# Loading four x tiles ahead of the v weights, projecting v of two of them early, and summing tile means on two engines, in the head of a one-core kernel

## The chip, the cores and the metric

One core of a Trainium2 chip runs the kernel. The metric is device time in microseconds (us). The names of the engines are: PE (TensorE, matrix products), ACT (ScalarE), DVE (VectorE), POOL (GpSimd), SP (SyncE, which here only issues transfers). Transfers are issued from two queues, SP's and ACT's.

## The reference

The input x has 2048 tokens of 512 numbers. It is normalised per token, and three things are added: x itself, a linear attention, and a bilinear gated layer.

```
xn  = (x - mean(x)) / sqrt(var(x) + 1e-5)
A   = linear_attention(xn @ wqkv, features = softmax(+-(q|k) @ w_phi), 32 heads of 16) @ wo
B   = ((xn @ w_gate) * (xn @ w_up)) @ w_down          # 512 -> 1792 -> 512
out = x + A + B
```

All inputs are bfloat16. The key and query parts of `wqkv` are folded with `w_phi` on the chip; the v part (`wv` below, 512 x 512) is used as it is.

## The kernel before: the parts that matter

x is worked on in 16 tiles of 128 tokens. A tile is centred (mean subtracted), transposed on PE, copied out of PSUM (the evacuation), and then multiplied with weights. For the first four tiles (ND = 4) the division by the standard deviation is deferred to later stages, so only the mean is on the path to the first matrix product. `sc.pin` keeps the recorded order on each engine; a small list scheduler orders everything else.

The transfers of the head:

```python
    sc.pin = True
    load_x(0, 2)                    # SP: x tiles 0 and 1
    load_v(SP, 0)                   # SP: rows 0-255 of wv ("half 0")
    load_x(2, 2)                    # SP: x tiles 2 and 3
    load_gu(SP, 0, (1,))            # SP: first slice of w_up
    act(sbf("lnv", 0, 1), eps_f, ["eps"], ["pace"])
    load_v(ACT, 1)                  # ACT: wv half 1
    load_gu(ACT, 0, (0,))           # ACT: first slice of w_gate
    load_gu(SP, 1)
    # ... w_phi, the transposed key weights, x tiles 4-7, more slices
```

The work of the head, in order (for one engine this order is kept):

```python
    warm(7)                         # matmuls on constants
    warm(2, 512, [("x", 0)])
    sc.pin = True
    ln_moments(0)                   # DVE: bn_stats + bn_aggr, gives the mean of tile 0
    ln_mean(1)                      # ACT: sum of tile 1 by accumulation
    ln_center(0, 2)                 # DVE
    ln_center(1, 2)
    x_transpose(0, 2, 0, 2)         # PE transposes, ACT or DVE copies out of PSUM
    x_transpose(0, 3, 1, 2)
    x_transpose(1, 4, 0, 2, DVE)
    x_transpose(1, 5, 1, 2, DVE)
    v_matmul(0, 0)                  # v of tile 0: half 0 of wv, then half 1
    v_matmul(1, 1)
    # ... ln_moments(2), ln_mean(3), centre tiles 2 and 3
    g0a()                           # quarter units of gate and up: 4 matmuls of 256 columns each
    x_transpose(2, 2)
    g1a()
    x_transpose(3, 3)
    u0a()
    u1a()
    sc.pin = False
    # ... the main loop follows; it computes v of tiles 2 to 15
```

The softmax here doesn't subtract the row's maximum and nothing guards it: scores larger than these inputs give would overflow.

Of the kernel before, what the change touches and what calls it, by code (L numbers as in the profile page):

```python
# [7 lines left out]
ACTF = mybir.ActivationFunctionType  # L8
# [7 lines left out]
H = 32  # L16
# [103 lines left out]
def _build(nc, es, A_x, A_wqkv, A_w_phi, A_wo, B_w_gate, B_w_up, B_w_down, out):  # L120
# [3 lines left out]
    def alloc(name, nelem, at=None):  # L124
        if at is not None:
            layout[name] = at
            return
        off = (cur[0] + 31) // 32 * 32
        layout[name] = off
        cur[0] = off + nelem  # L130
# [14 lines left out]
    alloc("ek", RK * 1024)  # L145
    alloc("vs", RK * H * HC)
    alloc("eq", RQ * 1024)
    alloc("o", 3 * 512)
    alloc("g", 4 * 512)
    alloc("ostg", 3 * 512)  # L150
# [9 lines left out]
    alloc("nbias", 2 * NT)  # L160
    alloc("lnv", 2 * NT)
    alloc("mu", 2 * ND)
    alloc("nrstd", 2 * ND)
    alloc("r2", 2 * ND)
    alloc("rpr", 2 * RK * 32)
# [20 lines left out]
    def sbf(name, lo, n):  # L186
        off = layout[name] + 2 * lo
        return arena[:, off:off + 2 * n].bitcast(F32)

    def bank(b, lo=0, n=512):  # L190
        return psum[:, b * 512 + lo:b * 512 + lo + n]
# [6 lines left out]
    def act(out_ap, in_ap, reads, writes, func=ACTF.Copy, scale=1.0, bias=None, accum=None):  # L198
        kw = {} if bias is None else {"bias": bias}
        if accum is not None:  # L200
            kw["accum_out"] = accum
        n = out_ap.free_size()
        return sc.step(ACT, lambda e: e.activation(out=out_ap, in_=in_ap, func=func, scale=scale, **kw),  # L203
                       reads, writes, 130.0 + 0.833 * n)

    def dve(fn, reads, writes, n, rate=1.04):
        return sc.step(DVE, fn, reads, writes, 140.0 + rate * n)
# [25 lines left out]
    def x_tile(t):  # L233
        return sb("x", t * 512, 512)
# [9 lines left out]
    def load_x(t0, n, eng=SP):  # L244
        o = sb("x", t0 * 512, n * 512).rearrange("p (t d) -> p t d", t=n)
        i = rows(x_flat, t0, n)
        sc.dma(eng, lambda e: e.dma_start(o, i), [], [("x", t) for t in range(t0, t0 + n)], n * 131072)
# [16 lines left out]
    def load_gu(eng, s, which=(0, 1)):  # L264
        lo, n = SLICES[s]
        sl = slice(lo, lo + n)
        for k in which:
            v, src = ((wg_v, B_w_gate), (wu_v, B_w_up))[k]
            load_w(eng, v[:, :, sl], src[:, sl].rearrange("(q p) f -> p q f", p=128), (("wg", "wu")[k], s),
                   1024 * n)  # L270

    def load_v(eng, h):
        i = A_wqkv[h * 256:(h + 1) * 256, 1024:1536].rearrange("(q p) j -> p q j", p=128)
        load_w(eng, wv_v[:, 2 * h:2 * h + 2, :], i, ("wv", h), 262144)
# [7 lines left out]
    pool(c_fn, [], ["const"], 300)  # L282

    sc.pin = True
    load_x(0, 2)
    load_v(SP, 0)
    load_x(2, 2)
    load_gu(SP, 0, (1,))
    act(sbf("lnv", 0, 1), eps_f, ["eps"], ["pace"])
    load_v(ACT, 1)  # L290
    load_gu(ACT, 0, (0,))
    load_gu(SP, 1)
    load_w(SP, wphi_v, bass.AP(tensor=A_w_phi.tensor, offset=A_w_phi.offset, ap=[[16, 128], [2048, NQ], [1, 16]]),
# [55 lines left out]
    def xn_tile(t):  # L349
        return sb("xn", (t % 4) * 512, 512)  # L350
# [8 lines left out]
    def ln_moments(t):  # L359
        dve(lambda e: e.bn_stats(stats_v[:, t, 0:6], x_tile(t)), [("x", t)], [("st", t)], 512)  # L360
        dve(lambda e: e.bn_aggr(mv_v[:, t, :], stats_v[:, t, 0:6]), [("st", t)], [("mv", t)], 1)  # L361
# [8 lines left out]
    def ln_stats(t0, n):  # L370
# [3 lines left out]
        ln_rstd(t0, n)  # L374
        sc.prio = 1

    def ln_mean(t):
        act(xn_tile(t), x_tile(t), [("x", t)], [("mu", t)], scale=1.0 / 512.0, accum=mu[:, t:t + 1])

# [53 lines left out]
    def features(name, t, w, b=None):  # L433
        s = t % (RK if w else RQ)
        e_v = sb(name, s * 1024, 1024).rearrange("p (h k f) -> p h k f", h=H, k=2)
        b = misc_bank() if b is None else b
        mm(bank(b), [(xnT(q, t * 128, 128), Wp_v[:, w, q, :]) for q in range(NQ)],
           xk(t) + [("Wp", w, q) for q in range(NQ)], b)
        src = bank(b).rearrange("p (h f) -> p h f", h=H)
        late = t < ND  # L440
        act(e_v[:, :, 0, :], src, [("ps", b)] + late * [("rstd", t)], [(name, s, 0)], func=ACTF.Exp,
            scale=rstd[:, t:t + 1] if late else 1.0)
        act(e_v[:, :, 1, :], src, [("ps", b)] + late * ["nrstd"], [(name, s, 1)], func=ACTF.Exp,
            scale=nrstd[:, t:t + 1] if late else -1.0)
        sr = t % 8 if w == 0 else 8 + t % 4
        sm = sums_v[:, sr]
        dve(lambda e: e.tensor_reduce(out=sm, in_=e_v, axis=AX.X, op=ALU.add),  # L447
            [(name, s, 0), (name, s, 1)], [("sums", sr)], 1024)
        rs = rs_v[:, s]
        if w == 1:  # L450
            dve(lambda e: e.reciprocal(out=rs, in_=sm), [("sums", sr)], [("rs", s)], 64, 6.5)  # L451
        else:
            dve(lambda e: e.reciprocal(out=rs[:, :, 1], in_=sm[:, :, 1]), [("sums", sr)], [("rs", s)], 32, 6.5)  # L453
        rat = rat_v[:, s]
        pool(lambda e: e.tensor_tensor(out=rat, in0=sm[:, :, 0], in1=rs[:, :, 1], op=ALU.mult),  # L455
             [("sums", sr), ("rs", s)], [("rat", s)], 32)
        pool(lambda e: e.tensor_tensor(out=e_v[:, :, 1, :], in0=e_v[:, :, 1, :],  # L457
                                       in1=rat[:, :, None].to_broadcast([128, H, 16]), op=ALU.mult),
             [(name, s, 1), ("rat", s)], [(name, s, 1)], 512)

    def vs_tile(t):
        return sb("vs", (t % RK) * H * HC, H * HC).rearrange("p (h c) -> p h c", h=H)

    def v_matmul(t, b, hs=(0, 1)):
        for h in hs:
            mm(bank(b), [(xnT(q, t * 128, 128), wv_v[:, q, :]) for q in (2 * h, 2 * h + 1)],
               ([("xnT", t, h)] if t < 2 else [("xnT", t)]) + [("wv", h)], b, start=h == 0, stop=h == 1)

    rpr_v = sbf("rpr", 0, RK * 32).rearrange("p (r h) -> p r h", r=RK)

    def v_scale(t, b):
        s = t % RK
        rp, key = rs_v[:, s, :, 0], ("rs", s)
        pool(lambda e, rp=rp: e.tensor_copy(out=vs_tile(t)[:, :, 16], in_=rp), [("rs", s)], [("vz", s)], 32)  # L474
        if t < ND:
            pr = rpr_v[:, s]
            pool(lambda e, rp=rp: e.tensor_scalar(out=pr, in0=rp, scalar1=rstd[:, t:t + 1], scalar2=None,
                                                  op0=ALU.mult), [("rs", s), ("rstd", t)], [("rpr", s)], 32)
            rp, key = pr, ("rpr", s)
        dve(lambda e: e.tensor_tensor(out=vs_tile(t)[:, :, 0:16], in0=bank(b).rearrange("p (h f) -> p h f", h=H),  # L480
                                      in1=rp.unsqueeze(2).to_broadcast([128, H, 16]), op=ALU.mult),
            [("ps", b), key], [("vs", s)], 512)

    def kv_acc(t):
        s = t % RK
# [150 lines left out]
    def warm(n, w=512, after=()):  # L636
        def fn(e):
            ins = None
            for _ in range(n):
                ins = e.matmul(bank(7, 0, w), lhsT=nc.const_aps.tensor(1.0, (128, 128), BF16),  # L640
                               rhs=nc.const_aps.tensor(1.0, (128, w), BF16), start=True, stop=True)
            return ins
        sc.step(PE, fn, after, [("ps", 7)], n * w * 0.8)

    warm(7)
    warm(2, 512, [("x", 0)])
    sc.pin = True
    ln_moments(0)
    ln_mean(1)
    ln_center(0, 2)  # L650
    ln_center(1, 2)
    x_transpose(0, 2, 0, 2)
    x_transpose(0, 3, 1, 2)
    x_transpose(1, 4, 0, 2, DVE)
    x_transpose(1, 5, 1, 2, DVE)
    v_matmul(0, 0)
    v_matmul(1, 1)
    ln_moments(2)
    ln_mean(3)
    ln_center(2)  # L660
    ln_center(3)
    ln_moments(1)
    ln_moments(3)
    (g0a, u0a, g0b, u0b), gate0 = up_unit(*ups.pop(0), pairs, 2)
    (g1a, u1a, g1b, u1b), gate1 = up_unit(*ups.pop(0), pairs, 2)
    g0a()
    x_transpose(2, 2)
    g1a()
    x_transpose(3, 3)
    u0a()  # L670
    u1a()
    sc.pin = False
    ln_deferred()
# [34 lines left out]
    for t in range(NT + 3):  # L708
        if t < NT:
            features("ek", t, 1)  # L710
        if t % 2 == 0 and 4 + t < NT:
            ln_stats(4 + t, 2)
        if t > 0:
            up()
        x_next(t + 4)
        late_loads(t)
        if 2 <= t - 1 < NT:
            b = misc_bank()
            v_matmul(t - 1, b)
            v_scale(t - 1, b)  # L720
        if t < 2:
            v_scale(t, t)
        else:
            up()
            if t >= 3:
                kv_acc(t - 3)
            if t < NT + 1:
                up()
        if 7 < t < 12:
            w_fold(0, t - 8)  # L730
        if t >= NT - 3:
            features("eq", t - NT + 3, 0)
            q_transpose(t - NT + 3)
# [164 lines left out]
```

## Time and profile before

221.38 us is the median of six runs (221.30 to 221.69). The traced run was taken apart from these and took 221.54 us.

| quantity | value | where it is read |
|---|---|---|
| PE busy | 98% of the span | the page |
| chain of waits on PE | 96% | the page |
| x tiles 0-1 have landed | 4.28 us | landings in the trace |
| first transpose | 5.59 us | timeline of PE |
| x tiles 2-3 have landed | 7.34 us | landings in the trace |
| PE without a gap from | 8.73 us | single matmuls in the trace |
| start of the last matmul | 217.29 us | single matmuls in the trace |

These are two lines of the page of the kernel before: the busy time of each engine, and the engines' shares of the chain that ended last.

```profile
PE 214.4 (98%) x1251; PEld 105.0 (48%) x1275; DVE 141.3 (64%) x245; ACT 86.2 (39%) x162; POOL 53.6 (24%) x119
PE 96%; DMA 2%; issue 1%; DVE 1%
```

PE is the bottleneck, nearly from end to end. (About two dozen matmul records are missing in this trace, so the sum of PE's busy time is not used for anything finer.) The question is where the last few per cent lie. The next lines are the chain of waits of the kernel before, in order of time: start, length, and what the chain ran through (pieces of under 0.1 us are left out).

```profile
0.79 3.49 DMA arena<-in_A_x_dram
4.30 0.71 DVE arena L360
5.03 0.19 DVE arena L361
5.25 0.30 DVE arena L385
5.59 0.87 PE ps L417 x8
6.46 2.22 PE ps L222 x12
8.73 0.40 PE ps L417 x4
```

Until 5.59 us the chain is a transfer (x tiles 0-1), bn_stats, its aggregation, and one half of the centring. From then on it stays on PE. The timeline of PE alone shows the gaps (start, busy time, line, shapes, number of matmuls; in brackets the idle time before them):

```profile
5.59 0.87 PE L417 MATMUL ps<-arena 128*128 128x128 bf16 x8 [0.66 <-DVE arena L385]
6.35 2.34 PE L222 MATMUL ps<-arena 128*128 128x512 bf16 x12
8.73 0.40 PE L417 MATMUL ps<-arena 128*128 128x128 bf16 x4
8.96 0.60 PE L222 MATMUL ps<-arena 128*128 128x256 bf16 x4
```

L417 is a transpose, L222 any product with a weight. The 0.2 us hole before 8.73 does not show as a wait in brackets, because the modelled ends of matmuls run on; it shows when the starts of single matmuls are compared. In a gapless stretch they follow each other by 216 ns (512 columns), 109 ns (256) or 56 ns (128).

That gives a way to count the head. Call *head cost* the time at which PE starts to run without a gap, less the real matmuls it has already done by then, at these spacings. Before: 8.73 us less 8 transposes, 8 v matmuls and 4 quarter matmuls (0.45 + 1.73 + 0.44 = 2.61 us) is 6.12 us.

### The profile page before, as it was taken

The numbers are of one execution on the slowest core, as the hardware profiler recorded it, in microseconds if no ns is written. First come the engines' busy times: TensorE is split into PE (matmuls) and PEld (weight loads), VectorE is DVE, ScalarE is ACT, GpSimd is POOL, SyncE is SP. The second block draws the span as 40 slices with busy tenths as digits, with TensorE's granted clock in tenths as the row PEclk, the third lists the DMA queues.
The fourth block names the chain that finished last, engine by engine and source line by source line (L and its number), as shares of the span: only waits on it lengthen the run. The fifth ranks groups of instructions, "written<-read, shape, count | busy, mean of one in ns | idle before, by whom it ended". The sixth has DMA issues, their size and how long they took to land.

```text
span 219.8 us, 3293 instructions
## 1 busy us (share of the span) xinstructions
PE 214.4 (98%) x1251; PEld 105.0 (48%) x1275; DVE 141.3 (64%) x245; ACT 86.2 (39%) x162; POOL 53.6 (24%) x119
## 2 busy tenths in 40 slices
PE   6999999999999999999999999999999999999995
PEld 1664444444444444544444444544454444454453
DVE  2766999876546654675486565797766777445341
ACT  4568774787343435333445525531122211000000
POOL 3030553332022202220241422224332222200000
DMA  6999715298200000000002220343764545342221
GB/s 182 295 302 297 198 43 121 59 336 185 49 0 0 0 3 0 0 0 3 0 0 48 49 47 4 71 74 76 163 144 100 118 106 115 87 102 73 61 61 49
DMA packets 47104, 19.90 MB, mean 91 GB/s; under 512 B 37488, under 2 KB 46448, under 8 KB 47088
## 3 DMA queue, kind: packets, MB, share of 16 engines
q1 hardware_dynamic: 46288, 19.16, 36.0%
q10 hardware_dynamic: 800, 0.52, 0.8%
q8 instruction: 10, 0.16, 0.3%
q14 instruction: 6, 0.05, 0.1%
HBM read 8.67 MB, written 2.10 MB: 49 GB/s over the span
## 4 chain that ended last, share of the span: by engine, by line
PE 96%; DMA 2%; issue 1%; DVE 1%
PE ps L222 91%; PE ps L539 2%; PE ps L492 2%; DMA arena<-in_A_x_dram 2%; PE ps L333 1%; PE ps L417 1%; DVE arena L360 0%; DVE arena L385 0%; DVE arena L621 0%; DVE arena L361 0%
## 5 line engine op out<-in xcount | busy, mean ns | idle before, releaser
L222 PE MATMUL ps<-arena 128*128 128x512 bf16 (+3 forms) x938 | 204.8, 371 | 1.3
L222 PEld LDWEIGHTS ps<-arena 128*128 128x128 bf16 x962 | 90.8, 98 | 98.2 <-ACT arena L203 0.2
L203 ACT ACTIVATE arena<-ps 128x512 bf16<-128x512 f32 (+2 forms) x114 | 63.0, 593 | 87.3 <-PE ps L222 74.3
L597 DVE TENSOR_TENSOR arena<-ps,arena 128x512 bf16<-128x512 f32 x56 | 38.5, 687 | 21.8 <-PE ps L222 18.0
L447 DVE TENSOR_REDUCE arena<-arena 128x64 f32<-128x1024 bf16 x32 | 38.5, 1213 | 20.9 <-ACT arena L203 20.9
L457 POOL TENSOR_TENSOR arena<-arena 128x512 bf16<-128x512 bf16 x32 | 33.9, 1060 | 1.3
L455 POOL TENSOR_TENSOR arena<-arena 128x32 f32<-128x32 f32 x32 | 8.6, 268 | 91.2 <-DVE arena L451 50.8
L621 DVE TENSOR_TENSOR arena<-ps,arena 128x512 bf16<-128x512 f32 (+2 forms) x13 | 8.5, 650 | 21.5 <-PE ps L222 21.5
L203 ACT ACTIVATE arena<-arena 128x512 bf16<-128x512 bf16 (+3 forms) x29 | 14.4, 508 | 5.8 <-DMA arena<-in_A_x_dram 2.8
L360 DVE BATCH_NORM_STATS2 arena<-arena 128x6 f32<-128x512 bf16 x16 | 10.4, 674 | 5.0 <-DMA arena<-in_A_x_dram 4.9
L203 ACT ACTIVATE arena<-ps,arena 128x512 bf16<-128x512 f32 x16 | 10.1, 685 | 5.7 <-PE ps L222 5.7
L560 DVE TENSOR_TENSOR arena<-ps,arena 128x512 bf16<-128x512 f32 x16 | 11.1, 691 | 0.6
L480 DVE TENSOR_TENSOR arena<-ps,arena 128x512 bf16<-128x512 f32 x16 | 10.3, 643 | 0.0
L451 DVE RECIPROCAL arena<-arena 128x64 f32<-128x64 f32 x16 | 8.4, 533 | 0.0
L492 PEld LDWEIGHTS ps<-arena 128*128 128x128 bf16 x128 | 6.2, 97 | 3.8
L539 PEld LDWEIGHTS ps<-arena 128*128 128x128 bf16 x128 | 6.2, 97 | 3.8
L397 POOL TENSOR_SCALAR arena<-arena 128x1 f32<-128x1 f32 x12 | 3.0, 269 | 17.7 <-ACT arena L203 17.7
L539 PE MATMUL ps<-arena 128*128 128x68 bf16 x128 | 6.7, 194 | 0.0
L492 PE MATMUL ps<-arena 128*128 128x68 bf16 x128 | 6.7, 194 | 0.0
L559 DVE RECIPROCAL arena<-arena 128x32 f32<-128x32 f32 x16 | 5.6, 353 | 0.5
L453 DVE RECIPROCAL arena<-arena 128x32 f32<-128x32 f32 x16 | 5.4, 344 | 0.2
L474 POOL CAST arena<-arena 128x32 bf16<-128x32 f32 x16 | 5.2, 322 | 0.0
(30 smaller groups left out, 34.0 us busy)
## 6 DMA issues: line engine op xcount, KB each, us to landing
out_dram<-arena SPq DMA_DIRECT2D x15, 128.0 KB, 1.7
arena<-in_B_w_down_dram SPq DMA_DIRECT2D x1, 1792.0 KB, 8.0
arena<-in_A_x_dram SPq DMA_DIRECT2D x3, 512.0 KB, 3.7
arena<-arena SPq DMA_TRANSPOSE x44, 2.8
arena<-in_B_w_gate_dram SPq DMA_DIRECT2D x1, 640.0 KB, 8.9
arena<-in_B_w_up_dram SPq DMA_DIRECT2D x1, 640.0 KB, 10.0
arena<-in_A_x_dram SPq DMA_DIRECT2D x2, 256.0 KB, 4.6
arena<-in_B_w_gate_dram SPq DMA_DIRECT2D x1, 512.0 KB, 5.4
```

The costliest lines, as they stand in the source:

```text
L203: return sc.step(ACT, lambda e: e.activation(out=out_ap, in_=in_ap, func=func, scale=scale, **kw), reads, writes, 130.0 + 0.833 * n)
L222: ins = e.matmul(out_ap, lhsT=l, rhs=r, start=start and i == 0, stop=stop and i == npair - 1, **kw)
L360: dve(lambda e: e.bn_stats(stats_v[:, t, 0:6], x_tile(t)), [("x", t)], [("st", t)], 512)
L447: dve(lambda e: e.tensor_reduce(out=sm, in_=e_v, axis=AX.X, op=ALU.add), [(name, s, 0), (name, s, 1)], [("sums", sr)], 1024)
L455: pool(lambda e: e.tensor_tensor(out=rat, in0=sm[:, :, 0], in1=rs[:, :, 1], op=ALU.mult), [("sums", sr), ("rs", s)], [("rat", s)], 32)
L457: pool(lambda e: e.tensor_tensor(out=e_v[:, :, 1, :], in0=e_v[:, :, 1, :], in1=rat[:, :, None].to_broadcast([128, H, 16]), op=ALU.mult), [ ...
L480: dve(lambda e: e.tensor_tensor(out=vs_tile(t)[:, :, 0:16], in0=bank(b).rearrange("p (h f) -> p h f", h=H), in1=rp.unsqueeze(2).to_broadca ...
L492: ins = e.matmul(bank(c // 4, (c % 4) * CW, CW), lhsT=ek[:, c * 128:(c + 1) * 128], rhs=vs[:, c * CW:(c + 1) * CW], start=(t == 0 and c % ...
L539: ins = e.matmul(bank(b0 + c // 4, (c % 4) * CW, CW), lhsT=ph[:, c, :], rhs=kvz_v[:, c, :], start=True, stop=True)
L560: dve(lambda e: e.tensor_tensor(out=o_tile(t).rearrange("p (b h f) -> p b h f", b=2, f=16), in0=nd[:, :, :, 0:16], in1=w_v[:, r].unsqueeze ...
L597: dve(lambda e: e.tensor_tensor(out=hT_v[:, ft, sg * 512:(sg + 1) * 512], in0=bank(bu), in1=g, op=ALU.mult), [("ps", bu), ("g", s)], [("hT ...
L621: dve(lambda e, ps=ps, stg=stg, cs=cs: e.tensor_tensor(out=stg, in0=ps, in1=x_tile(t)[:, cs], op=ALU.add), [("ps", bk), ("x", t)], [("ostg ...
```

## The change

Its intent is to start PE's real work earlier and give it more to do early. The first x transfer is cut in two, on two queues; all four first x tiles go ahead of `wv`; the mean of a tile is summed half on ACT and half on DVE; and v of tiles 2 and 3 is projected in the head, where it is copied raw in float32 into a buffer that is free until late, and scaled in the loop.

```diff
-    load_x(0, 2)
-    load_v(SP, 0)
+    load_x(0, 1)
+    load_x(1, 1, ACT)
     load_x(2, 2)
+    load_v(SP, 1)
     load_gu(SP, 0, (1,))
     act(sbf("lnv", 0, 1), eps_f, ["eps"], ["pace"])
-    load_v(ACT, 1)
+    load_v(ACT, 0)
     load_gu(ACT, 0, (0,))
@@ new helpers
+    def ln_mean_split(t):      # ACT sums columns 256-511, DVE columns 0-255
+    def ln_center_split(t):    # DVE, two halves, subtracts both part means
+    def ln_center_whole(t):
+    def v_keep(t, b):          # ACT: PSUM -> float32 in SBUF
@@ head
-    warm(2, 512, [("x", 0)])
+    warm(1, 512, [("x", 0)])
-    ln_moments(0)
-    ln_mean(1)
-    ln_center(0, 2)
-    ln_center(1, 2)
+    ln_mean_split(0)
+    ln_center_split(0)
+    ln_mean_split(1)
+    ln_center_split(1)
+    ln_mean_split(2)
     x_transpose(0, 2, 0, 2)
     x_transpose(0, 3, 1, 2)
+    warm(1, 256)
     x_transpose(1, 4, 0, 2, DVE)
     x_transpose(1, 5, 1, 2, DVE)
+    warm(1, 256)
+    ln_center_whole(2)
+    ln_mean(3)
+    ln_center(3)
     v_matmul(0, 0)
-    v_matmul(1, 1)
-    ... statistics of tiles 0 to 3
+    v_matmul(1, 1, (0,))
+    x_transpose(2, 6)
+    v_matmul(1, 1, (1,))
+    for t in range(ND):
+        ln_moments(t)
     g0a()
-    x_transpose(2, 2)
-    g1a()
-    x_transpose(3, 3)
-    u0a()
+    x_transpose(3, 7)
+    v_matmul(2, 2)
+    v_keep(2, 2)
+    u0a()
+    v_matmul(3, 3)
+    v_keep(3, 3)
+    g1a()
     u1a()
@@ loop: v of tiles 2 and 3 is scaled from the kept copy, no matmul there
```

More of the change, by code (lines that the diff above doesn't have):

```diff
@@ L147, in _build @@
     alloc("eq", RQ * 1024)
+    alloc("vraw", 2 * 1024, at=layout["eq"])
     alloc("o", 3 * 512)
@@ L162, in _build @@
     alloc("mu", 2 * ND)
+    alloc("mua", 2 * ND)
     alloc("nrstd", 2 * ND)
@@ L375, in ln_stats @@
         sc.prio = 1
+    mua = sbf("mua", 0, ND)
+    def ln_mean_split(t):
+        act(xn_tile(t)[:, 256:], x_tile(t)[:, 256:], [("x", t)], [("mu", t)], scale=1.0 / 512.0,
+            accum=mu[:, t:t + 1])
+        dve(lambda e: e.tensor_scalar(out=xn_tile(t)[:, :256], in0=x_tile(t)[:, :256], scalar1=1.0 / 512.0,
+                                      scalar2=0.0, op0=ALU.mult, op1=ALU.add, accum_out=mua[:, t:t + 1]),
+            [("x", t)], [("mua", t)], 256)
+    def ln_center_split(t):
+        for h in range(2):
+            hs = slice(h * 256, (h + 1) * 256)
+            dve(lambda e, hs=hs: e.tensor_scalar(out=xn_tile(t)[:, hs], in0=x_tile(t)[:, hs], scalar1=mua[:, t:t + 1],
+                                                 scalar2=mu[:, t:t + 1], op0=ALU.subtract, op1=ALU.subtract),
+                [("x", t), ("mua", t), ("mu", t)], [("xn", t, h)], 256, 0.27)
+    def ln_center_whole(t):
+        dve(lambda e: e.tensor_scalar(out=xn_tile(t), in0=x_tile(t), scalar1=mua[:, t:t + 1],
+                                      scalar2=mu[:, t:t + 1], op0=ALU.subtract, op1=ALU.subtract),
+            [("x", t), ("mua", t), ("mu", t)], [("xn", t, 0)], 512, 0.27)
     def ln_mean(t):
@@ L440, in features @@
         late = t < ND
-        act(e_v[:, :, 0, :], src, [("ps", b)] + late * [("rstd", t)], [(name, s, 0)], func=ACTF.Exp,
+        over = [("vraw", 2), ("vraw", 3)] if name == "eq" and t < 2 else []
+        act(e_v[:, :, 0, :], src, [("ps", b)] + late * [("rstd", t)], [(name, s, 0)] + over, func=ACTF.Exp,
             scale=rstd[:, t:t + 1] if late else 1.0)
@@ L467, in v_matmul @@
                ([("xnT", t, h)] if t < 2 else [("xnT", t)]) + [("wv", h)], b, start=h == 0, stop=h == 1)
+    def v_keep(t, b):
+        raw = sbf("vraw", (t - 2) * 512, 512)
+        act(raw, bank(b), [("ps", b)], [("vraw", t)])
     rpr_v = sbf("rpr", 0, RK * 32).rearrange("p (r h) -> p r h", r=RK)
@@ L479, in v_scale @@
             rp, key = pr, ("rpr", s)
-        dve(lambda e: e.tensor_tensor(out=vs_tile(t)[:, :, 0:16], in0=bank(b).rearrange("p (h f) -> p h f", h=H),
+        src, skey = (bank(b), ("ps", b)) if b is not None else (sbf("vraw", (t - 2) * 512, 512), ("vraw", t))
+        dve(lambda e: e.tensor_tensor(out=vs_tile(t)[:, :, 0:16], in0=src.rearrange("p (h f) -> p h f", h=H),
                                       in1=rp.unsqueeze(2).to_broadcast([128, H, 16]), op=ALU.mult),
-            [("ps", b), key], [("vs", s)], 512)
+            [skey, key], [("vs", s)], 512)
     def kv_acc(t):
@@ L645, in _build @@
     warm(7)
-    warm(2, 512, [("x", 0)])
+    warm(1, 512, [("x", 0)])
     sc.pin = True
-    ln_moments(0)
-    ln_mean(1)
-    ln_center(0, 2)
-    ln_center(1, 2)
+    ln_mean_split(0)
[3 more added lines that the diff above has]
+    ln_mean_split(2)
     x_transpose(0, 2, 0, 2)
     x_transpose(0, 3, 1, 2)
+    warm(1, 256)
     x_transpose(1, 4, 0, 2, DVE)
     x_transpose(1, 5, 1, 2, DVE)
+    warm(1, 256)
+    ln_center_whole(2)
+    ln_mean(3)
+    ln_center(3)
     v_matmul(0, 0)
-    v_matmul(1, 1)
-    ln_moments(2)
-    ln_mean(3)
-    ln_center(2)
-    ln_center(3)
-    ln_moments(1)
-    ln_moments(3)
+    v_matmul(1, 1, (0,))
[3 more added lines that the diff above has]
+        ln_moments(t)
     (g0a, u0a, g0b, u0b), gate0 = up_unit(*ups.pop(0), pairs, 2)
@@ L716, in _build @@
         late_loads(t)
-        if 2 <= t - 1 < NT:
+        if 2 <= t - 1 < ND:
+            v_scale(t - 1, None)
+        elif ND <= t - 1 < NT:
             b = misc_bank()
```

## The prediction

> **What bounds the kernel now.** TensorE (PE). The page gives PE 98% of the span, the chain of waits 96% PE. In the timeline, single matmuls follow each other by 216 ns (512 columns), 109 (256) or 56 (128). The program's real matmuls multiplied by these spacings give, as my estimate, about 211 us, and the last one ends near 217.5 us. So PE loses time almost only in the head, and every 0.1 us there is 0.1 us of the whole; later stages have no slack that could be gained. From 8.73 us on PE runs without a gap; the real work done by then (8 transposes, v of tiles 0 and 1, 4 gate matmuls) is 2.6 us, so the head costs about 6.1 us. It is: x tiles 0-1 land at 4.28 us (transfer landings in the trace), statistics 0.69 + 0.18 us and centering end at about 5.5, transposes 5.59 to 6.35 (in pairs, 0.07 us lost four times), then v from 6.35, and a 0.20 us gap at 8.5 where transpose 2 waits for x tiles 2-3, which land only at 7.35.
>
> **What the change does.** It removes from the path: half of the first x transfer, bn_stats of tiles 0 and 2 (0.69 + 0.18 each, moved later), one long warm-up matmul. It adds two 256-column warm-ups (0.1 us each), two-engine half sums (estimate from the 512-wide 0.63 + 0.18 us on ScalarE: about 0.4 + 0.18), and two copies of v of tiles 2 and 3 to SBUF on ScalarE (0.60 us each, an engine that is 55-70% busy there). It moves 8 v matmuls (1.7 us) from the loop into the head; PE work in sum is unchanged. It moves both wv halves behind x.
>
> **Where the path goes.** The Trainium skill (Trainium Kernel Development and Optimization, Key Constraints) says that transfers issued from different queues share the same 16 DMA engines and interleave. The trace agrees: ACT's first wv half lands at 4.99 us, between SP's x (4.28) and second wv half (5.76), at 330 to 390 GB/s together. So x first means wv later. Estimates from those landings: x0 3.5, x1 3.7, x2-3 4.8, wv half 0 5.5, half 1 about 6.2, first gate and up slices about 7 and 8.2 (their total bytes are unchanged). Transposes 0 and 1 go at about 4.5 to 5. But in engine order the half sum of tile 2 precedes the evacuation of transpose 0 on ScalarE, so that waits for x2: evacuated about 5.8 to 6.1. v of tile 0, second half, then starts at about 6.3, and PE should run on without a gap, with 0.9 us of real work done: head cost about 5.4 us, against 6.1. I take off 0.1 for small new gaps.
>
> Gain about 0.6 us of 221.39: **220.8 us**, range 220.0 to 221.5. Chances: faster by over 2% 0.01, within 2% 0.98, slower by over 2% 0.01.
>
> **What would show it.** Right: first transpose near 4.5 us; first v matmul near 5.8, waiting for the evacuation or wv, no longer for statistics; no PE gap after about 6.6; last matmul about 0.6 us earlier; PE busy about unchanged. Wrong steps: wv half 1 landing after 6.7; gaps before the first gate or up matmuls (weights late).
>
> **What would make it wrong.** wv or gate weights later than estimated eat the gain. Evacuations of transposes 2 and 3 late behind other ScalarE work would stall v 2 and 3. The seven first warm-ups run 427 ns apart, later matmuls 216: if the thinner head let the clock fall back, it would cost over 1 us. A reshuffled order on ScalarE or VectorE could open gaps in the loop. If wv comes faster than I think, up to 1.3 us is gained.

## The result, and the profile after

The changed kernel took 221.57 us (median of six, 221.33 to 221.71), against 221.38 before. The ratio is 1.0005, with a 95% interval of 0.9992 to 1.0018. (Ratios are the mean time of one kernel's runs over that of the other's of the same rounds, so they are not quite the ratio of the medians.) A second measurement of the same kernel, told below, gave 1.0037 (1.0012 to 1.0062). So the change is worth nothing, or a little less than nothing; the forecast gain of 0.6 us did not come.

The page of the changed kernel, the same two lines:

```profile
PE 215.8 (98%) x1276; PEld 105.3 (48%) x1276; DVE 143.0 (65%) x251; ACT 87.6 (40%) x168; POOL 53.7 (24%) x119
PE 96%; DMA 2%; SPq 0%; issue 0%; DVE 0%
```

The chain of waits of the changed kernel, in order of time:

```profile
0.79 0.39 SPq L249
1.24 0.41 SPq L249
1.70 5.16 DMA arena<-in_A_wqkv_dram
7.00 1.02 PE ps L224 x4
8.02 0.22 PE ps L441 x4
```

The beginning of the chain is another one. Before, it was x and its statistics. Now it is the SP queue issuing two x transfers, then one transfer of `wv` which takes 5.16 us from issue to landing, and then PE. Statistics are off the path, as intended; the transfer that was put behind x is on it. PE's timeline in the changed kernel (L441 transposes, L670 warm-ups, L224 products):

```profile
4.60 0.54 PE L441 MATMUL ps<-arena 128*128 128x128 bf16 x4 [0.20 <-DVE arena L392]
5.58 0.54 PE L441 MATMUL ps<-arena 128*128 128x128 bf16 x4 [0.32 <-DVE arena L392]
6.06 0.59 PE L224 MATMUL ps<-arena 128*128 128x512 bf16 x2
7.00 1.02 PE L224 MATMUL ps<-arena 128*128 128x512 bf16 x4 [0.34 <-DMA arena<-in_A_wqkv_dram]
7.86 0.39 PE L441 MATMUL ps<-arena 128*128 128x128 bf16 x4
```

The first transpose starts 1 us earlier, the first product 0.3 us earlier; then PE stops after two matmuls, half 0 of v of tile 0, and waits for half 1 of `wv`. From 7.00 us on there is no gap at all. But by then only 8 transposes and 2 matmuls (0.45 + 0.43 us) are done. The head cost is 7.00 - 0.88 = 6.12 us, in these two traces the same to the hundredth, and the last matmul starts at 217.28 us instead of 217.29. Both head costs are 211.16 to 211.17 us ahead of that last start, so nothing after the head gained or lost. That they agree to the hundredth is chance: the traced run of the kernel before (221.54 us) was 0.16 us slower than the median of its six, while that of the changed kernel (221.57) was at its median. As an estimate from this difference, a usual run of the kernel before has a head cost nearer to 5.96 us.

Where `wv` was delayed can be read from the transfers. These lines are some of the transfers issued in the first 4 us, before and then after: what, queue, size, and the median time from issue to landing.

```profile
arena<-in_A_x_dram SPq DMA_DIRECT2D x2, 256.0 KB, 4.6
arena<-in_A_wqkv_dram ACTq DMA_DIRECT2D x1, 256.0 KB, 4.1
arena<-in_A_wqkv_dram SPq DMA_DIRECT2D x1, 256.0 KB, 4.5
arena<-in_B_w_gate_dram ACTq DMA_DIRECT2D x1, 256.0 KB, 5.2
```

```profile
arena<-in_A_x_dram SPq DMA_DIRECT2D x1, 256.0 KB, 3.8
arena<-in_A_wqkv_dram ACTq DMA_DIRECT2D x1, 256.0 KB, 4.4
arena<-in_A_wqkv_dram SPq DMA_DIRECT2D x1, 256.0 KB, 5.2
arena<-in_B_w_gate_dram ACTq DMA_DIRECT2D x1, 256.0 KB, 6.0
arena<-in_A_x_dram SPq DMA_DIRECT2D x1, 128.0 KB, 2.8
```

The later of the two `wv` halves landed at 5.76 us before and at 6.86 us after. The same 1.5 MB are brought in the head in both kernels, and both have the last of it (the first up slice) at 8.2 to 8.5 us. The change only dealt out anew which part comes first.

A transfer is carried by up to 16 engines, and is complete when the last share has landed. The Trainium skill says so (DMA: Bandwidth & Descriptors, "Why a DMA increments its semaphore by 16 and not by 1"), and the trace agrees: each transfer here has 16 landings. For `wv` half 1 in the changed kernel they are, in us:

```
5.46 5.49 5.57 5.79 5.81 5.92 5.98 5.99 6.00 6.03 6.06 6.29 6.38 6.39 6.52 6.86
```

Half of it is there at 5.99 us. PE waits for the last share, 0.87 us later.

### The profile page after: what moved, and what is told of

It is laid out like the page before. It is cut to its first block, busy times and chain, and to the rows that moved or that the text cites. A ratio compares the mean times of both kernels' runs of the same rounds, so it can differ in the third digit from the quotient of the medians.

```text
span 219.8 us, 3329 instructions
## 1 busy us (share of the span) xinstructions
PE 215.8 (98%) x1276; PEld 105.3 (48%) x1276; DVE 143.0 (65%) x251; ACT 87.6 (40%) x168; POOL 53.7 (24%) x119
## 4 chain that ended last, share of the span: by engine, by line
PE 96%; DMA 2%; SPq 0%; issue 0%; DVE 0%
PE ps L224 91%; DMA arena<-in_A_wqkv_dram 2%; PE ps L569 2%; PE ps L522 2%; PE ps L336 1%; SPq L249 0%; PE ps L441 0%; DVE arena L651 0%
## 5 line engine op out<-in xcount | busy, mean ns | idle before, releaser
L224 PE MATMUL ps<-arena 128*128 128x512 bf16 (+3 forms) x962 | 207.2, 371 | 0.3 <-DMA arena<-in_A_wqkv_dram 0.3
L224 PEld LDWEIGHTS ps<-arena 128*128 128x128 bf16 x962 | 90.9, 98 | 98.4 <-ACT arena L205 0.8
L205 ACT ACTIVATE arena<-ps 128x512 bf16<-128x512 f32 (+3 forms) x116 | 64.4, 594 | 87.6 <-PE ps L224 74.5
L627 DVE TENSOR_TENSOR arena<-ps,arena 128x512 bf16<-128x512 f32 x56 | 38.3, 686 | 20.9 <-PE ps L224 17.1
L205 ACT ACTIVATE arena<-arena 128x512 bf16<-128x512 bf16 (+4 forms) x31 | 14.6, 495 | 4.1 <-DMA arena<-in_A_x_dram 1.9
L590 DVE TENSOR_TENSOR arena<-ps,arena 128x512 bf16<-128x512 f32 x16 | 11.1, 692 | 0.6
L510 DVE TENSOR_TENSOR arena<-ps,arena 128x512 bf16<-128x512 f32 x14 | 9.0, 641 | 0.0
L580 POOL TENSOR_SCALAR arena<-arena 128x32 f32<-128x32 f32 x4 | 1.2, 291 | 16.3 <-DVE arena L472 16.3
```

Source lines behind the costliest of these rows:

```text
L205: return sc.step(ACT, lambda e: e.activation(out=out_ap, in_=in_ap, func=func, scale=scale, **kw), reads, writes, 130.0 + 0.833 * n)
L224: ins = e.matmul(out_ap, lhsT=l, rhs=r, start=start and i == 0, stop=stop and i == npair - 1, **kw)
L510: dve(lambda e: e.tensor_tensor(out=vs_tile(t)[:, :, 0:16], in0=src.rearrange("p (h f) -> p h f", h=H), in1=rp.unsqueeze(2).to_broadcast([ ...
L590: dve(lambda e: e.tensor_tensor(out=o_tile(t).rearrange("p (b h f) -> p b h f", b=2, f=16), in0=nd[:, :, :, 0:16], in1=w_v[:, r].unsqueeze ...
L627: dve(lambda e: e.tensor_tensor(out=hT_v[:, ft, sg * 512:(sg + 1) * 512], in0=bank(bu), in1=g, op=ALU.mult), [("ps", bu), ("g", s)], [("hT ...
```

## The experiments

Theory A: the head lasts until the last transfer that PE's next product needs, and whatever the head costs, the whole costs. The wait for `wv` half 1 gave back what the earlier x had won. Theory B: the order of work on ACT costs the time, because it evacuates transpose 0 only after the half sum of tile 2. Theory C: the head does not count, later stages absorb it.

### Filling the wait with other work: e1_order

```diff
-    v_matmul(0, 0)
+    v_matmul(0, 0, (0,))
     v_matmul(1, 1, (0,))
+    v_matmul(0, 0, (1,))
     x_transpose(2, 6)
```

> The changed kernel, but TensorE multiplies the first half of v of tile 1 before the second half of v of tile 0. Theory A (TensorE stood from 6.50 to 7.00 us for wv half 1, which lands at 6.86, and this wait gave back what the earlier x won): the wait is filled with 0.43 us of work, the wait before 7.00 shrinks to under 0.1 us, and the last matmul starts about 0.43 us earlier than in the changed kernel (16.85 before 217.28 reads 216.85); time about 221.1. Theory B (the late evacuation of the transposes behind the half sum of tile 2 costs the time): the first half of v of tile 1 would wait as well, gain under 0.15 us. Theory C (later stages absorb what the head wins): the head is shorter, but the time stays within 0.1 us of the changed kernel.

221.69 us (221.31 to 221.82), so no gain: here the expectation of theory A missed. PE's timeline of this run shows why:

```profile
5.99 1.03 PE L224 MATMUL ps<-arena 128*128 128x512 bf16 x4
7.24 0.59 PE L224 MATMUL ps<-arena 128*128 128x512 bf16 x2 [0.23 <-DMA arena<-in_A_wqkv_dram]
7.67 0.39 PE L441 MATMUL ps<-arena 128*128 128x128 bf16 x4
7.89 1.25 PE L224 MATMUL ps<-arena 128*128 128x512 bf16 x6
```

The first half of v of tile 1 did fill the wait (four matmuls in a row, without a stop, so theory B is wrong). But in this run `wv` half 1 landed at 7.11 us, with the same transfers as in the changed kernel, and the gate slice, which travels at the same time on the other queue, only at 8.49 instead of 7.72 us: a new gap of 0.21 us opened before the first gate matmul at 8.54. The head cost is 6.14 us. Two things follow: landings vary from run to run by some tenths of a us, and behind one late transfer stands another.

### Taking the gate slice out of the way: e2_wg_later

```diff
     load_v(SP, 1)
+    load_gu(SP, 0, (0,))
     load_gu(SP, 0, (1,))
     act(sbf("lnv", 0, 1), eps_f, ["eps"], ["pace"])
     load_v(ACT, 0)
-    load_gu(ACT, 0, (0,))
```

> The changed kernel, but the first gate slice is issued on the SP queue behind wv half 1, so that it no longer shares the DMA engines with it. Theory A: wv half 1 lands at about 6.2 instead of 6.86 us, the second half of v of tile 0 starts at about 6.5 instead of 7.00, gate slice 0 lands by 7.8 (needed at about 8.0), time about 0.4 us less than the changed kernel, 221.1. Theory B: no change, within 0.15 us. If wv half 1 still lands after 6.7, it was not the sharing with the gate slice that delayed it.

This run took 221.13 us (221.06 to 221.19); ratio to before 0.9976 (0.9949 to 1.0004; the runs of the kernel before had outliers up to 223.04, which widen it). `wv` half 1 landed at 6.43 us and the gate slice at 7.33. The transfers and PE's timeline of this run:

```profile
arena<-in_A_wqkv_dram SPq DMA_DIRECT2D x1, 256.0 KB, 4.7
arena<-in_B_w_gate_dram SPq DMA_DIRECT2D x1, 256.0 KB, 5.2
```

```profile
5.60 0.63 PE L441 MATMUL ps<-arena 128*128 128x128 bf16 x4
6.04 0.29 PE L670 MATMUL ps<-const-bfloat16-1.0 128*128 128x256 bf16 x1
6.17 1.46 PE L224 MATMUL ps<-arena 128*128 128x512 bf16 x6
7.46 0.39 PE L441 MATMUL ps<-arena 128*128 128x128 bf16 x4
```

How the two queues shared the engines shows between 5.5 and 6.5 us: queue, packets, MB moved, and packets' time as a share of the 16 engines' (q10 is ACT's queue, q1 is SP's). The first two lines are of the changed kernel, the third is the only one of this run:

```profile
q10 hardware_dynamic: 414, 0.21, 71.9%
q1 hardware_dynamic: 164, 0.10, 34.0%
q1 hardware_dynamic: 668, 0.35, 114.3%
```

In the changed kernel two thirds of what was moved in that us came from ACT's queue, mainly the gate slice, while PE was about to wait for `wv` half 1 on SP's queue. In this run SP's queue had the engines to itself.

Six matmuls follow each other from 6.17 us, where the changed kernel stopped after two. The head cost is 5.72 us, the last matmul starts 0.39 us earlier than in the changed kernel (216.89), and the median is 0.44 us less than the changed kernel's of the first measurement. Theory A said 0.4. Theory C is wrong: what the head wins, the whole wins. Against the kernel before, the medians differ by less, 0.22 us (221.35) where the head costs of the traces differ by 0.40, mainly because the traced run of the kernel before (221.54) was slower than most of its runs. The gate slice even came sooner than in the changed kernel (7.33 against 7.72 us), though its issue was later and on the busier queue. The Trainium skill says that transfers from several queues run on the same 16 engines and interleave, and that a second issuing engine only saves issue time (DMA: Bandwidth & Descriptors, "Issuing engines are not separate DMA queues"). This agrees: the first up slice, last of the same 1.5 MB, landed at 8.21 us here, 8.22 in the kernel before and 8.52 in the changed one.

### The order on ACT and DVE: e3_sum2_later

```diff
     ln_center_split(1)
-    ln_mean_split(2)
     x_transpose(0, 2, 0, 2)
     ...
     x_transpose(1, 5, 1, 2, DVE)
     warm(1, 256)
+    ln_mean_split(2)
```

> The changed kernel, but the half sums of tile 2 stand behind the evacuations of transposes 0 and 1 in the order of ScalarE and VectorE. Theory A: ScalarE evacuates transpose 0 at about 5.0 instead of 5.49, the first v matmul still starts only after transpose 1 and wv half 0 (5.63), near 6.06, and the second half still waits for wv half 1 to 6.9 to 7.0; time the same within 0.1 us. Theory B (this order costs the time): at least 0.3 us faster.

221.82 us (221.35 to 221.99). ACT evacuated transpose 0 at 4.96 instead of 5.49 us, and it bought nothing: `wv` half 1 landed at 7.04 us in the traced run, its first matmul started at 7.18, and the last matmul is 0.18 us later than in the changed kernel, as the landing is. Theory B is out. It was an item of the prediction that this evacuation sets the start; it does not.

### Leaving v of tiles 2 and 3 in the loop: e4_v_in_loop

```diff
     x_transpose(3, 7)
-    v_matmul(2, 2)
-    v_keep(2, 2)
     u0a()
-    v_matmul(3, 3)
-    v_keep(3, 3)
     g1a()
     ...
-        if 2 <= t - 1 < ND:
-            v_scale(t - 1, None)
-        elif ND <= t - 1 < NT:
+        if 2 <= t - 1 < NT:
```

> The changed kernel, but v of tiles 2 and 3 stays in the loop as before (not projected early, no copy in SBUF). Theory A says the early v of tiles 2-3 stands behind the wait for wv half 1 and in front of weights that have landed (up slice 0 at 8.52, needed at 9.2 without it), so it buys nothing: no new gap on TensorE after 7.0, time within 0.1 us of the changed kernel. A rival (the early v covers late gate and up weights) says a new gap of up to 0.5 us before the first up matmuls and a time 0.3 to 0.5 us longer.

222.14 us (221.48 to 223.61), which is outside of what either theory said. The trace has no new gap after the one wait for `wv`, which is longer here:

```profile
6.03 0.59 PE L224 MATMUL ps<-arena 128*128 128x512 bf16 x2
7.67 1.02 PE L224 MATMUL ps<-arena 128*128 128x512 bf16 x4 [1.05 <-DMA arena<-in_A_wqkv_dram]
```

Half 1 landed at 7.54 us, and 7.67 less 0.88 us is a head cost of 6.79. So the extra time is the landing, in this trace. (The run of 223.61 us is another matter: its granted clock was 0.992, that of the other five 1.0.) Whether v in the loop makes the landing later, or whether it was a bad round, this run alone cannot say. Two runs below say it was not v in the loop.

### First attempt to beat both kernels: e5_wv_first

```diff
     load_x(0, 1)
     load_x(1, 1, ACT)
-    load_x(2, 2)
     load_v(SP, 1)
+    load_x(2, 2)
+    load_gu(SP, 0, (0,))
     load_gu(SP, 0, (1,))
     ...
     load_v(ACT, 0)
-    load_gu(ACT, 0, (0,))
@@ PE's order
+ transpose 0, v of tile 0 with wv half 0, transpose 1, v of tile 0 with half 1, v of tile 1,
+ g0a, transpose 2, g1a, transpose 3, u0a, v of tile 2, u1a, v of tile 3
@@ tile 2's half sums behind the evacuations of transposes 0 and 1
```

> Meant to beat both kernels. The changed kernel with both wv halves issued ahead of x tiles 2-3, the first gate slice behind those on the SP queue, tile 2's half sums behind the evacuations of transposes 0 and 1, and TensorE's order: transpose 0, v of tile 0 first half, transpose 1, rest of v of tiles 0 and 1, first gate quarter, transpose 2, and so on. Theory A (the head lasts as long as its last-landing weight makes it, and every 0.1 us of it is 0.1 us of the whole): wv halves land at about 5.2, first v matmul at about 5.35 instead of 6.06, no wait over 0.15 us after it, head cost about 5.1 us, last matmul near 216.3, time about 220.5. If the first gate slice (about 7.3) or transposes 2-3 come late, a gap of 0.1 to 0.3 us shows and the gain is smaller by it. Theory C (later stages absorb the head's gain): time stays above 221.0 though the head is shorter.

221.24 us (220.85 to 221.34), ratio 0.9992 (0.9979 to 1.0005). The traced run is the one of 220.85: first product at 5.42 us, a gap of 0.17 us before the first gate matmul at 7.55 (the gate slice landed at 7.51), head cost 5.37, last matmul at 216.55. That is what theory A asked for, but three of the five runs were 0.4 to 0.5 us longer. Products now start as soon as `wv` half 0 lands, so no slack is left to hide a late share; in e2 the first product stood behind transpose 1 anyway, half a us after its weight had landed, and its six runs lie within 0.13 us. That missing slack makes the times spread is not shown, and e12 and e11 below speak against it.

### Gate slice out of the way, v in the loop: e6_wg_later_v_loop

This is e2 and e4 together.

> The run with the gate slice behind wv half 1, but v of tiles 2 and 3 left in the loop. Theory A: wv half 1 lands near 6.43 again, TensorE runs without a gap from about 6.1, the up slice (8.2) is there when it is needed (8.4 to 8.6), so the time is that of the run with early v, 221.1, within 0.1: the early v buys nothing. If the long time of the run with v in the loop (222.14) was due to v in the loop itself and not to that run's late landing of wv half 1 (7.54), this one is 0.4 us or more slower than 221.1.

221.16 us (221.14 to 221.19), as e2. `wv` half 1 landed at 6.42 us and the head cost is 5.66. So the early v and its two float32 copies buy nothing, and the long time of e4 was not caused by v in the loop.

### Only the split of the first x transfer: e7_x_split

```diff
-    load_x(0, 2)
+    load_x(0, 1)
+    load_x(1, 1, ACT)
```

This is on the kernel before.

> The kernel before, but its first x transfer split in two: tile 0 on the SP queue, tile 1 on the ACT queue; nothing else. Theory A: tiles 0 and 1 land at 3.5 to 3.7 instead of 4.28, transposes start near 4.8 instead of 5.59, v near 5.8 (wv half 0, and statistics no longer on the path), but x tiles 2-3 still land at 7.0 to 7.35, so that transpose 2 still starts near 8.4 to 8.7 behind a gap of 0.4 to 0.7 us: time within 0.2 us of before. A rival that the first transposes' start alone sets the head's length says 0.7 us faster.

221.40 us (221.20 to 221.75), the same as before, within the 0.2 us that theory A allowed. But the reason it gave was wrong in part. x tiles 2-3 landed at 6.74 us and were not what PE waited for; the gap of 0.30 us stood before the first gate matmul at 7.80, because the gate slice landed at 7.76. The traced run (221.20, the fastest) has a head cost of 5.62. Once one limit of the head is moved, the next transfer in the line becomes the limit.

### Only the changed loads: e8_loads_only

```diff
-    load_x(0, 2)
-    load_v(SP, 0)
+    load_x(0, 1)
+    load_x(1, 1, ACT)
     load_x(2, 2)
+    load_v(SP, 1)
     ...
-    load_v(ACT, 1)
+    load_v(ACT, 0)
```

The compute is that of the kernel before.

> The kernel before with only the changed order of loads (x tiles 0, 1, 2-3 first, then wv; halves on the changed kernel's queues), its compute untouched. Theory A: wv half 1 lands at 6.9 to 7.5 as in the changed kernel, v's second half starts right after, so the time equals the changed kernel's, 221.4 to 221.7: the two-engine sums and the early v have no part in the result. If the two-engine sums do pay, this run is at least 0.3 us slower than the changed kernel.

221.75 us (221.27 to 222.46), 0.05 us above what was expected, ratio to before 1.0023 (1.0008 to 1.0038): as slow as the changed kernel, without any of its compute. Half 1 landed at 6.97 us. PE's timeline:

```profile
4.76 0.88 PE L418 MATMUL ps<-arena 128*128 128x128 bf16 x8 [0.47 <-DVE arena L386]
5.78 0.59 PE L222 MATMUL ps<-arena 128*128 128x512 bf16 x2
7.10 1.24 PE L222 MATMUL ps<-arena 128*128 128x512 bf16 x5 [0.73 <-DMA arena<-in_A_wqkv_dram]
```

It is the changed kernel's picture: two matmuls, then the wait for half 1 of `wv`. The eight transposes even come earlier (the last one starts at 5.42 us) than the changed kernel's, whose second four only begin at 5.58. With the old statistics DVE sums tile 0 while ACT sums tile 1; with the split sums, DVE takes part in both, one after the other, and the pair is ready later.

### A second attempt, and the changed kernel again: e9_one_queue and e10_again

e9 is e5 with these loads, with transpose 2 ahead of the first gate quarters, and with the first up quarter behind v of tile 2:

```diff
     load_x(0, 1)
     load_x(1, 1, ACT)
+    load_v(SP, 0)
     load_v(SP, 1)
-    load_x(2, 2)
+    load_x(2, 1)
     load_gu(SP, 0, (0,))
+    load_x(3, 1)
     load_gu(SP, 0, (1,))
     ...
-    load_v(ACT, 0)
```

> A second attempt to beat both kernels, after the first one's times spread from 220.85 to 221.34. Only x tile 1 stays on the ACT queue; the SP queue carries x tile 0, wv halves 0 and 1, x tile 2, first gate slice, x tile 3, first up slice, so that from wv on no two queues share the DMA engines; TensorE takes transpose 2 ahead of the first gate quarters. If it is the sharing of the engines by two queues that makes the last of the 16 shares of a transfer late and its time vary, wv half 0 lands at about 4.6 and half 1 at 5.4, the first v matmul starts when transpose 0 is evacuated (about 5.3), no gap over 0.15 us follows, the last matmul is near 216.3 and all runs lie near 220.6 within 0.2 us of each other. If the spread has another cause, the runs spread as before, over 0.4 us.

> The changed kernel once more, unaltered, beside the one above. Theory A: its times again lie between 221.3 and 221.8 and follow the landing of wv half 1, which falls between 6.8 and 7.2 us in the traced run; last matmul between 217.2 and 217.6.

e9 took 221.00 us (220.75 to 221.34), ratio 0.9984 (0.9971 to 0.9997). `wv` landed early (4.37 and 5.17 us) and the first product started at 5.27, but PE then had gaps of 0.11 us (transpose 2), 0.31 us (transpose 3, at 8.77, behind the sum of tile 3 on ACT, which could start only when that tile landed at 7.51) and 0.17 us at 13.5. The runs still spread over 0.59 us. So a single queue does not by itself make the times steady, and the expectation that it would has failed. No transfer was under way on the other queue when this run's gate slice travelled, and its last two shares still landed at 6.74 and 7.14 us, the other fourteen by 6.28.

e10, the changed kernel unaltered, took 221.94 us (221.37 to 223.72), ratio 1.0037 (1.0012 to 1.0062). In its traced run half 1 landed at 7.38 us, and the last matmul started at 217.80, both later than expected; so were four of the six times, which lie above 221.8 us. One of them, 223.72, had a granted clock of 0.992; without it the ratio of the means is still 1.0023.

```profile
6.22 0.72 PE L224 MATMUL ps<-arena 128*128 128x512 bf16 x2
7.52 1.02 PE L224 MATMUL ps<-arena 128*128 128x512 bf16 x4 [0.58 <-DMA arena<-in_A_wqkv_dram]
```

So the landing at 6.86 us in the first trace is an early one for these loads, and that of e4 (7.54 us) is not far beyond what the changed kernel itself shows.

### The gaps taken out: e11_no_gap

```diff
-    ln_mean_split(2)
-    ln_center_whole(2)
-    ln_mean(3)
-    ln_center(3)
+    ln_mean(2)                                    # ACT alone
+    ln_center_by(2, mu[:, 2:3], ("mu", 2))
     ...
-    for t in range(ND):
-        ln_moments(t)
+    ln_moments(3)                                 # bn_stats on DVE gives tile 3's mean
+    ln_center_by(3, mv_v[:, 3, 0:1], ("mv", 3))
+    for t in range(3):
+        ln_moments(t)
     ...
-    x_transpose(3, 3)
     v_matmul(2, 2)
+    x_transpose(3, 3)
     v_keep(2, 2)
```

This is on e9; the new helper `ln_center_by`, which subtracts a given mean, is left out.

> The one-queue run with its two remaining gaps on TensorE (0.11 us before transpose 2, 0.31 us before transpose 3) taken out: the mean of tile 2 is summed by ScalarE alone as soon as tile 2 lands, that of tile 3 by bn_stats on VectorE, and transpose 3 stands behind v of tile 2. Theory A: first v matmul again near 5.27, no gap over 0.15 us after it, last matmul near 216.4 instead of 216.85, time about 220.6, at least 0.2 us less than the one-queue run. Theory C (later stages absorb): time as the one-queue run, 221.0.

220.68 us (220.50 to 221.04), ratio 0.9970 (0.9957 to 0.9984). It beats both kernels. PE's timeline:

```profile
4.53 0.65 PE L446 MATMUL ps<-arena 128*128 128x128 bf16 x4
5.40 0.60 PE L224 MATMUL ps<-arena 128*128 128x512 bf16 x2
5.84 0.39 PE L446 MATMUL ps<-arena 128*128 128x128 bf16 x4
6.06 1.47 PE L224 MATMUL ps<-arena 128*128 128x512 bf16 x6
7.37 0.39 PE L446 MATMUL ps<-arena 128*128 128x128 bf16 x4
7.60 1.90 PE L224 MATMUL ps<-arena 128*128 128x256 bf16 x12
```

From 5.40 us on there is no gap, with 0.22 us of work done: head cost 5.18 us, last matmul at 216.36.

### The repaired loads on the kernel before: e12_loads_fixed

The loads of e2, the compute of the kernel before.

> The kernel before, compute untouched, with the load order of the run that put the first gate slice behind wv half 1 on the SP queue. Theory A: wv half 1 lands near 6.43, its matmul starts near 6.55, last matmul within 0.15 us of that run's 216.89, time 221.1 to 221.2: the whole gain over the kernel before comes from the loads, and neither the two-engine sums nor the early v is needed for it. If the two-engine sums pay once wv is in time, this run is 0.3 us or more slower than 221.13.

221.08 us (221.02 to 221.13), ratio 0.9987 (0.9975 to 1.0000). `wv` half 1 landed at 6.31 us, its first matmul started at 6.44 after a wait of 0.31 us, head cost 5.56, last matmul 216.72. e2's whole gain is in the order of the loads; split sums and early v are not needed for it, and the simpler compute is, if anything, a little ahead in the trace.

### All runs in one table

"last share" is the landing of `wv` half 1 in the traced run, "8th" that of its eighth share. Head cost as defined above. These and the last matmul are of the traced run, whose own time stands beside them; it need not be near the median of all runs.

| run | 8th, last share of wv half 1 | head cost | last matmul | traced run us | median us (range) |
|---|---|---|---|---|---|
| before | (half 0: 5.31, 5.76) | 6.12 | 217.29 | 221.54 | 221.38 (221.30-221.69) |
| changed | 5.99, 6.86 | 6.12 | 217.28 | 221.57 | 221.57 (221.33-221.71) |
| e1_order | 6.00, 7.11 | 6.14 | 217.31 | 221.62 | 221.69 (221.31-221.82) |
| e3_sum2_later | 5.85, 7.04 | 6.30 | 217.46 | 221.77 | 221.82 (221.35-221.99) |
| e4_v_in_loop | 6.34, 7.54 | 6.79 | 217.96 | 222.25 | 222.14 (221.48-223.61) |
| e8_loads_only | 6.26, 6.97 | 6.22 | 217.39 | 221.77 | 221.75 (221.27-222.46) |
| e10_again | 6.40, 7.38 | 6.64 | 217.80 | 222.09 | 221.94 (221.37-223.72) |
| e2_wg_later | 5.97, 6.43 | 5.72 | 216.89 | 221.19 | 221.13 (221.06-221.19) |
| e6_wg_later_v_loop | 6.01, 6.42 | 5.66 | 216.84 | 221.15 | 221.16 (221.14-221.19) |
| e12_loads_fixed | 5.90, 6.31 | 5.56 | 216.72 | 221.02 | 221.08 (221.02-221.13) |
| e5_wv_first | last 4.98 (half 0: 5.28) | 5.37 | 216.55 | 220.85 | 221.24 (220.85-221.34) |
| e7_x_split | last 5.54 | 5.62 | 216.81 | 221.20 | 221.40 (221.20-221.75) |
| e9_one_queue | last 5.17 | 5.50 (+0.17 later) | 216.85 | 221.13 | 221.00 (220.75-221.34) |
| e11_no_gap | last 5.34 | 5.18 | 216.36 | 220.72 | 220.68 (220.50-221.04) |

Last matmul less head cost is 211.16 to 211.19 us in every row (for e9 with its later gap added), whatever the kernel, and the time of the traced run is 4.25 to 4.39 us more than the start of its last matmul. So what the head costs, the whole costs, as theory A has it. The kernel before, run again, had medians of 221.30 to 221.38 us.

No run differs from the kernel before by as much as 2%. The 95% intervals of the ratios are clear of 1 for e8 and e10 (slower) and for e9 and e11 (faster). For e2, e6 and e12 they reach 1, but every one of their runs was shorter than every run of the kernel before in the same call (221.19 against 221.20 us, 221.19 against 221.21, 221.13 against 221.23).

With the gate slice of the other queue beside it (changed kernel, e1, e3, e4, e8, e10), the last share of `wv` half 1 lands 0.71 to 1.20 us after the eighth; with the gate slice behind it (e2, e6, e12), 0.40 to 0.46 us. The eighth share itself comes at 5.85 to 6.40 us in the one group and 5.90 to 6.01 in the other, so it is above all the tail, from the eighth share to the last, that is longer. That three of three runs differ from six of six in this way is shown; why shares lag is open. Having a neighbour on the other queue is not the whole of it: in the kernel before, `wv` half 0 travelled beside the gate slice too, with a tail of 0.46 us, and e9's gate slice had a tail of 1.00 us with nothing on the other queue. Open as well is why the runs of e5, e9 and e11 spread over about half a us. Little slack is not enough as a reason: in the trace of e11 each weight of the head landed 0.7 us or more before its first product, and its runs spread over 0.54 us; e12 waited for its half 1, and its runs lie within 0.11 us.

## Why the prediction was right or wrong

- That PE bounds the kernel, that only the head can be gained, and that 0.1 us there is 0.1 us of the whole: right. The constant 211.17 us of the table shows it. The forecast that the effect would be far below 2% was therefore right too, though the measured time lies just above the stated range (221.57 against 221.5), and "last matmul about 0.6 us earlier" did not come (217.28 against 217.29).
- That x would land at 3.5, 3.7 and 4.8 us: nearly right (3.55, 3.72, 5.05). The first transpose near 4.5: right (4.60); the first product near 5.8: 0.26 us late (6.06). No gap after the start of the second half of v: right (none after 7.00), but it was to start by about 6.6. That PE's matmuls stay at their short spacing: right (56 ns at 4.98 us and 216 ns from 6.06 on). The Trainium skill (TensorE: Matmul & The Clock Gate, Part 1) says that about 3.4 us of busy time bring on the full clock. The traces fit: the warm-up matmuls start at 0.83 us and stand 427 ns apart up to 3.76 us; in the kernel before, the two that start at 4.32 us stand 228 ns apart.
- That the evacuation of transpose 0, behind the half sum of tile 2, would set the start of v: wrong. PE's own order put transpose 1 (second half at 5.83 us) ahead of v, and e3, which took the evacuation's wait away, gained nothing.
- The step that failed, as the prediction put it, is "half 1 about 6.2": the landing of `wv` half 1. The mechanism was named (x first means `wv` later, PE would wait for it), but the term was mis-sized. It measured 6.86 us in the first trace and 6.97 to 7.54 us in five more with the same loads. The forecast series for half 1, first gate and first up slice (6.2, 7, 8.2) is close to what e2 measured with the three in line on one queue (6.43, 7.33, 8.21). In the changed kernel the gate slice was on the other queue and took its share of the engines in the meantime, though the prediction itself said that queues interleave: 6.86, 7.72, 8.52. The forecast was also near the time of the eighth share (5.85 to 6.40 us), but PE waits for the last. The head cost was forecast at 5.4 us and was 6.12 in the first trace, 6.12 to 6.79 over all six.
- That early v and split sums would belong to the gain: the prediction did not separate them. e8 and e12 (neither of them) and e6 (no early v) show that they had no part in the result. Of the "0.1 for small new gaps" nothing came.
- Among the things that "would make it wrong" stood "wv or gate weights later than estimated eat the gain". That is what happened.

## What to carry to other kernels

When one engine is busy from end to end, count its head as start of gapless work less the work already done; a change that starts the engine earlier but lets it stop once more before the same amount of work is done has moved nothing. Order the first transfers by what the busy engine needs next, all of them together: putting one forward puts another back, since the bytes are the same, and a wait ends with the last of 16 shares, not with the mean. Leave a transfer that work waits for without a competitor on the other queue: in the three runs that did so with the changed order of loads (e2, e6, e12), half 1 landed 0.4 to 1.2 us earlier than in the six that did not. And look at several runs before believing one trace, and at where the traced run lies among them.

## What the Trainium skill lacked or had wrong

- DMA: Bandwidth & Descriptors says that the engines of one transfer finish independently, but gives no size for it: here the last of 16 shares of one 256 KB transfer (`wv` half 1) came 0.17 to 1.20 us after the eighth in the fourteen traces, where a gain of 0.6 us was at stake.
- The same page says that issuing from a second engine only saves issue time. In total that agrees (the same 1.5 MB had landed at 8.09 to 8.47 us in the six runs with the gate slice on SP's queue and at 8.22 to 8.93 us in the eight with it on ACT's), but it does not say how much later a transfer lands for having company on the other queue: `wv` half 1 landed at 6.31 to 6.43 us with the gate slice queued behind it and at 6.86 to 7.54 us with it on the other queue.
- No page has the cost of summing half a tile on VectorE by its accumulator, as measured here: 0.42 us for 256 columns and 0.08 us for reading the sum, against 0.69 and 0.18 us for bn_stats of 512 columns and its aggregation. For two tiles in a row the split over two engines was no gain (second four transposes from 5.58 us, against all eight started by 5.42 us with the old statistics on the same loads).
